# The high and low parts of z1 and z2 queued at the end of the pair two ahead, and the Gelus of two products behind the copies

## The chip, the cores and the metric

The kernel runs on one core of one Trainium2 chip. The metric is the device time of one execution in microseconds (us), of which the median of three runs is given: 945.27 us, from 944.91 to 945.61.

## What is computed

The reference is one layer on x (2048 x 512, float32): a Fourier mixing and then a gated MLP.

```python
h = _layernorm(x) * (1 + ca) + sa
x = x + ga * _A_ref(h, ...)            # (Cr h) Hr - (Ci h) Hi
h = _layernorm(x) * (1 + cb) + sb
z = _gelu(h @ w_in)                    # 2048 x 1792
z1, z2 = z[..., :896], _layernorm(z[..., 896:])
g = w_sp @ z2 + b_sp[:, None]          # w_sp is 2048 x 2048
out = x + gb * ((z1 * g) @ w_out)
```

The six vectors sa to gb come from silu(c) @ w_mod.

## The kernel before, in words

Every product runs in float32 from two rounded parts of each operand. The **high part** is a copy in a rounded type, made by ScalarE (ACT, `ah`, line 278). The **low part** is what the copy lost, made by VectorE (DVE, `al`, line 296). TensorE (PE) then runs three matmuls: high by high, high by low, low by high (lines 95 to 97).

The program is written in stages. First come the Fourier products (`gp`, `yp`, tiles numbered 0 to 127). Then come z1 = gelu(h w1) (`z1p`, tiles 128 to 155) and z2 = gelu(h w2) (`z2p`, tiles 156 to 183), then w_sp times z2 (`gw`, tiles from 184), then the output product (`op`). z1, z2 and w_sp are each done as seven products of half-size blocks instead of eight (Strassen's scheme), in the order YPROD = 1, 2, 6, 7, 4, 5, 3 for z1, and ZPROD = 1, 6, 7, 4, 5, 3, 2 for z2.

In z1 and z2 a product takes two **pairs** of moving tiles. Pair n is tiles n and n+1 (n even), so z1 has the pairs 128, 130, ... 154 and z2 the pairs 156, ... 182. A pair of z1 is 18 matmuls into three banks of PSUM (`z1p`), besides some groups of six into a fourth (`f7p`). A pair of z2 is 24 matmuls into four banks (`z2p`). A product that goes on adding to a bank needs the old sum copied out first, or put back in.

Four kinds of work stand on ACT and DVE around a pair:

- Forming the tile. For products 6 of z1 and 1 and 2 of z2 the tile is first a sum or difference on DVE (`form_t`; `s2` in line 241, `t` in line 247). For product 7 of z1 it is the first half of h with `s2` added to it (`sum_x11`, line 253, in the tiles `xb`).
- The high part (`prep_hi`, ACT) and the low part (`prep_lo`, DVE). The pools hold four high parts (`ah`, bufs=4) and three low ones, with a slot for the fourth. So the high part of tile n+4 goes where that of tile n was, and has to wait until pair n has run.
- The weights' high and low parts, one per product: `vj` (lines 633 and 637) in z1, `wj` (lines 669 and 673) in z2, in two buffers.
- Emptying the banks (`empty_z1`, `empty_z`). Products 1, 6 and 7 copy the sums out on ACT (lines 737, 771). Products 2 and 4 apply the Gelu (lines 699, 773). Products 5 and 3 add on DVE (lines 743, 775) and then apply the Gelu on ACT (lines 701, 778). After product 2 of z1 and within product 3 of z2, ACT puts an older sum back into the bank (lines 730 and 777).

The order on each engine is the order in which the program is written (`manual_schedule`). `prep(n)`, at the head of the loop's step n, queues the high part of tile n+3 and the low part of n+2, and the even steps also the low part of n+3. So the parts of pair n+4 come behind everything that empties pair n. The table `fill` (`at(n, f, ...)`, run by `run(n)`) puts the rest in: the weights' parts, the sums of w_sp's blocks (`sum_s`, `sj`), the layernorm of z2 (`norm_z`, statistics on DVE and GpSimd; `scale_z`, ACT, line 119), the parts of w_sp's first four tiles (`first`, tiles 184 to 187) and the first parts of z2 as an operand (`hi_b`, `lo_b`, called `bh` and `bl`).

Of the kernel before, what the change touches and what calls it, by code (L numbers as in the profile page):

```python
# [8 lines left out]
F32 = mybir.dt.float32  # L9
# [4 lines left out]
P = 128  # L14
# [5 lines left out]
def fnet_gmlp_kernel(  # L20
# [36 lines left out]
    Q = 512  # L57
# [8 lines left out]
    def pool(name, side="left", bufs=1):  # L66
        return tc.tile_pool(name=name, bufs=bufs, side=side, reuse_waits="tile")
# [6 lines left out]
    blocks = ctx.enter_context(pool("blocks"))  # L74
# [48 lines left out]
    def at(n, f, *a):  # L123
        fill.setdefault(n, []).append((f, a))
# [6 lines left out]
    def quad(a, r, k):  # L131
        return a[r * Q:(r + 1) * Q, k * Q:(k + 1) * Q]
# [6 lines left out]
    N2 = 4 * len(src)  # L139
    YPROD = (1, 2, 6, 7, 4, 5, 3)  # L140
    NY = {p: N2 + 4 * i for i, p in enumerate(YPROD)}
    N3 = N2 + 4 * len(YPROD)
    ZPROD = (1, 6, 7, 4, 5, 3, 2)
    NZ = {p: N3 + 4 * i for i, p in enumerate(ZPROD)}
    N4 = N3 + 4 * len(ZPROD)
# [3 lines left out]
    NB0 = len(src) + 2  # L149
    stage, T, AH, AL = {}, {}, {}, {}  # L150
# [14 lines left out]
    def load(b):  # L165
# [10 lines left out]
        elif 4 * (b - NB0) < NE - N4:  # L176
# [4 lines left out]
            for r in range(2):  # L181
                load_half(stage[b][:, r], s_d[S_OF[p], r, g] if p in S_OF else
                          quad(w_sp, r + (2 if p == 4 else 0), g + (2 if p == 1 else 0)), h)

    def squares(dst, block, k):
        nc.vector.transpose(dst.rearrange("p (b i) -> p b i", i=32), block[:, :, 32 * k:32 * k + 32])  # L186

# [9 lines left out]
    def slot(i, name, dtype=F32):  # L197
        return slots[0].tile([P, Q], dtype, tag=f"slot{i}", bufs=1, name=name)
# [56 lines left out]
    highs, lows, SE = set(), set(), []  # L255
# [8 lines left out]
    def prep_hi(n):  # L264
        if n >= NE or n in highs:
            return
        highs.add(n)
        if N2 <= n < N4:
            T[n] = form_t(n)
        else:  # L270
            b, k = divmod(n, 4) if n < N2 else (NB0 + (n - N4) // 4, (n - N4) % 4)
            T[n] = SE[1][:, k] if b == NB0 else blocks.tile([P, Q], F32, tag="t", bufs=2, name=f"t{n}")
            if n >= N4:
                squares(T[n], stage[b][:, k % 2], k // 2)
            else:
                squares(T[n], stage[b], k)
        AH[n] = SE[2][:, n - N4] if N4 <= n < N4 + 4 else blocks.tile([P, Q], F32R, tag="ah", bufs=4, name=f"ah{n}")
        nc.scalar.activation(AH[n], T[n], AF.Copy)  # L278
        if not N2 <= n < N4 and k == 3:
            stage.pop(b)  # L280
            if b != NB0:
                load(b + 2)


    def prep_lo(n):
        if n >= NE or n in lows:
            return
        lows.add(n)
        if N2 <= n < N4 and n % 4 == 3:
            AL[n] = slot(0, f"al{n}", F32R) if slots else zrow[0].tile([P, Q], F32R, tag="z1u", bufs=6, name=f"al{n}")  # L290
        elif N4 <= n < N4 + 4:
            AL[n] = slot(9 + n - N4, f"al{n}", F32R)
        else:
            AL[n] = blocks.tile([P, Q], F32R, tag="al", bufs=3, name=f"al{n}")
        t = T.pop(n)
        nc.vector.tensor_tensor(AL[n], t, AH[n].bitcast(F32), op=ALU.subtract)  # L296
        gg, kk = divmod(n % 4, 2)
        if NY[7] <= n < NY[7] + 4:
            nc.vector.tensor_tensor(TT[2 + kk, gg], TT[2 + kk, gg], S2[gg, kk], op=ALU.subtract)
# [302 lines left out]
    z_hi, z_lo, Z, ZN = {}, {}, {}, {}  # L602
# [61 lines left out]
    def w_of(p):  # L664
        return parts_w2()[{1: 0, 6: 0, 7: 1, 5: 1, 2: 2, 4: 0, 3: 3}[p]]
# [5 lines left out]
    def lo_w(p):  # L671
        hi, lo = WJ[p][:, 0, :, :ZP], WJ[p][:, 1, :, :ZP]
        nc.vector.tensor_tensor(lo, w_of(p), hi.bitcast(F32), op=ALU.subtract)

    ZB = (0, 1, 2, 6, 3, 4, 5, 7)
    Z1 = {}

    def mm_f7(g, k, th, tl):

        if k == 0:  # L680
            ZT["f7", g] = bank(6 + g % 2, f"f7p{g}")
        matmul3(ZT["f7", g], W7[0][:, 0, k], W7[0][:, 1, k], th, tl, k == 0, k == ND - 1)
        if k == ND - 1:
            end_z1(g, NF - 1, ZT.pop(("f7", g)), out_row(g, NF - 1))
# [9 lines left out]
    def turned(z):  # L694
        return z.rearrange("p (k a i) -> p k a i", k=4, i=32)
# [12 lines left out]
    def mm_z1(n):  # L708
        p = YPROD[(n - N2) // 4]
        gg = n % 4 // 2  # L710
        fresh = p in (1, 5)
        a = [(AH.pop(m), AL.pop(m)) for m in (n, n + 1)]
        if p in (2, 3):
            for kk, t in enumerate(a):
                mm_f7(gg if p == 2 else 2 + gg, 2 + kk, *t)
        for f in range(3):
            if fresh:
                ZT[gg, f] = bank(3 * gg + f, f"z1p{p}_{gg}{f}")
            cols = slice(f * P, (f + 1) * P)
            for kk, (th, tl) in enumerate(a):  # L720
                matmul3(ZT[gg, f], WJ[1, p][:, 0, kk, cols], WJ[1, p][:, 1, kk, cols], th, tl,
                        fresh and kk == 0, kk == 1, not fresh)
        for f in range(3):
            empty_z1(p, gg, f)
        if p == 1:
            for kk, t in enumerate(a):
                mm_f7(gg, kk, *t)
        if p == 2:
            for f in range(3):
                nc.scalar.activation(turned(ZT[gg, f]), natural(Z1.pop((1, gg, f))), AF.Copy)  # L730
# [15 lines left out]
    def mm_z2(n):  # L746
        p = ZPROD[(n - N3) // 4]
        gg = (n - N3) % 4 // 2
        fresh = p in (1, 5)
        a = [(AH.pop(m), AL.pop(m)) for m in (n, n + 1)]  # L750
        for r in range(4):
            q = 4 * gg + r
            ts = slice(r * P, (r + 1) * P)
            if fresh:
                ZT[q] = bank(ZB[q], f"z2p{p}_{q}")
            for kk, (th, tl) in enumerate(a):
                matmul3(ZT[q][:, :ZP], th[:, ts], tl[:, ts], WJ[p][:, 0, kk, :ZP], WJ[p][:, 1, kk, :ZP],
                        fresh and kk == 0, kk == 1, not fresh)
        empty_z(p, gg)

    def empty_z(p, gg):

        qs = range(4 * gg, 4 * gg + 4)
        for q in qs:
            if p in (1, 7):
                s = q + (8 if p == 1 else 0)
                Z[s] = zpool[s // 8].tile([P, FH], F32, name=f"z2_{s}")
            z = Z[q + (8 if p in (1, 6, 3, 2) else 0)]
            ps = ZT[q][:, :ZP]
            if p in (1, 6, 7):  # L770
                nc.scalar.activation(z[:, E0 if p == 1 else E1], ps, AF.Copy)
            elif p in (2, 4):
                nc.scalar.activation(z[:, E0], ps, AF.Gelu_apprx_tanh)
            else:
                nc.vector.tensor_tensor(z[:, E1], ps, z[:, E1], op=ALU.add)
                if p == 3:
                    nc.scalar.activation(ps, z[:, E0], AF.Copy)
                nc.scalar.activation(z[:, E1], z[:, E1], AF.Gelu_apprx_tanh)

    def norm_z(s):  # L780
# [56 lines left out]
    def mm_w(n):  # L837
# [4 lines left out]
        if k == 0 and fresh:  # L842
            for f in range(nf):
                GW[r, f] = bank(ZB[4 * r + f], f"gw{p}_{r}_{f}")
        ah, al = AH.pop(n), AL.pop(n)
# [157 lines left out]
    for s, n in ((4, 4), (5, 4), (6, 6), (7, 6), (8, 10), (9, 10)):  # L1003
        m = n + (s == 9)
# [23 lines left out]
    for j, turn, weigh, row, fold, hi in ((0, (25, 26, 27, 28), (29, 29, 30, 30), 26, (34, 34, 35, 36), (38, 35, 36, 37)),  # L1028
# [8 lines left out]
        n = weigh[3] + (3 if j == 0 else 1)  # L1037
# [13 lines left out]
    for t in range(NQ):  # L1051
        n = 8 * NQ * (t + 1)
# [86 lines left out]
    for n in range(N2, N3):  # L1139
        prep(n)  # L1140
        if n % 2 == 0:
            prep_lo(n + 3)
        run(n)
        if n % 2 == 0:
            mm_z1(n)
            if n == N2:
                prep_hi(N2 + 4)
                prep_hi(N2 + 5)
                norm_y(NQ - 1, 3)
                prep_lo(N2 + 4)  # L1150
                prep_lo(N2 + 5)
                post_h(NQ - 1, 3)
                turn_h(NQ - 1, 3)
                change_s()
                zout.append(w0.enter_context(pool("zout")))
            if n in (N2 + 6, N2 + 10):
                mm_x((n - N2) // 10)
# [9 lines left out]
    at(N3 + 6, form_w, 4)  # L1167
    at(N3 + 8, load_first)
    for k in range(4):
        at(N3 + 12 + k, prep_hi, N4 + k)  # L1170
        at(N3 + 13 + k, prep_lo, N4 + k)
    at(N4 - 8, load, NB0 + 1)
    at(N4 - 3, load, NB0 + 2)
    for i, p in enumerate(PROD):
        for k in range(8):
            n = NB[p] + 2 * k
            early = 1 if p == 1 and k == 0 else 0
            at(n - (3 if p == 1 else 4) - early, hi_b, p, k)
            at(n - 2 - early, lo_b, p, k)
            if p == 1:  # L1180
                at(n - (10 if k == 0 else 5), norm_z, k)
                at(n - (7 if k == 0 else 4), scale_z, k)
                at(n + 6, norm_z, 8 + k)
                at(n + 7, scale_z, 8 + k)
                at(n + 10, sum_t23, k)
            if p == 4:
                at(n - 5, sum_t14, k)
    for f in range(NF):
        n = N4 + 24 + 8 * f
# [4 lines left out]
    for n in range(N3, N4):  # L1194
        prep(n)
        if (n - N3) % 2 == 0:
            prep_lo(n + 3)
        run(n)
        if (n - N3) % 2 == 0:
            mm_z2(n)  # L1200

    opool = []

# [93 lines left out]
```

## Time and profile before

| | |
|---|---|
| median of three runs | 945.27 us (944.91 to 945.61) |
| the profiled execution's own time | 945.57 us |
| its span, first to last instruction | 943.8 us |
| mean granted clock of TensorE | 0.999 |
| busy: PE, DVE, ACT, GpSimd (POOL) | 934.0, 738.4, 413.9, 195.1 us |
| z1 on PE | from 448.50 to 517.17 us |
| z2 on PE | from 517.17 to 591.14 us |

A row of the timeline has the start in us from the span's start, the duration, the engine, the line of the kernel, the operation, out<-in by the program's names (without buffer numbers), the shapes and how many like it stand in a row (x2, x3). In brackets stands the engine's idle time before it, and what ended it. Matmuls overlap, so the time of one is the distance from its start to the next one's, not its duration.

### The profile page before, as it was taken

Reading aid. Unit: us, or ns where it says so; the run is one execution under the profiler, and the core shown is the slowest. Engines: PE = TensorE matmul, PEld = TensorE weight load, DVE = VectorE, ACT = ScalarE, POOL = GpSimd, SP = SyncE. Lnnn points to the kernel's source line nnn. Section 1 sums busy time; section 2 is a strip of 40 time slices with the busy share of each in tenths; the row PEclk is TensorE's granted clock in tenths of the full one; section 3 lists DMA queues with packets and bytes.
Section 4 is the critical chain, followed back from the end, with each engine's and each line's share of the span. In section 5 each row is a group of like instructions: output and inputs, shape, how many; then the busy total and the mean of one; then the engine's idle time right before and its main releaser. Section 6 shows DMA issues by size and latency. Waiting matters only on the chain.

```text
span 943.8 us, 12366 instructions
## 1 busy us (share of the span) xinstructions
PE 934.0 (99%) x4114; PEld 771.6 (82%) x4114; DVE 738.4 (78%) x1201; ACT 413.9 (44%) x726; POOL 195.1 (21%) x372
## 2 busy tenths in 40 slices
PE   8999999999999999999999998999999999999998
PEld 5888888888888888888878996888888888888886
DVE  7789957777677677866898878799799889886662
ACT  4685424232132222322686867675545444331221
POOL 2330000114553165323524200332000000000000
PEclk9999999999999999999999999999999999999999
DMA  9995762647539977994787422344554465743541
GB/s 210 221 222 123 140 145 67 167 134 189 136 101 319 272 214 209 280 334 157 232 305 275 158 69 63 93 94 105 137 133 114 108 150 134 183 110 143 182 175 57
DMA packets 236592, 157.07 MB, mean 166 GB/s; under 512 B 131472, under 2 KB 203408, under 8 KB 236400
## 3 DMA queue, kind: packets, MB, share of 16 engines
q1 hardware_dynamic: 223008, 118.65, 50.5%
q0 software_dynamic: 12128, 37.11, 10.9%
q8 instruction: 32, 0.52, 0.2%
q10 hardware_dynamic: 1392, 0.52, 0.2%
q14 instruction: 32, 0.26, 0.1%
HBM read 119.54 MB, written 36.70 MB: 166 GB/s over the span
## 4 chain that ended last, share of the span: by engine, by line
PE 93%; ACT 3%; DVE 2%; issue 1%; DMA 1%; POOL 0%; SPq 0%; DVEq 0%; ACTq 0%
PE gp L97 12%; PE gp L95 12%; PE gp L96 12%; PE gw L97 10%; PE gw L95 10%; PE gw L96 10%; PE yp L95 3%; PE yp L97 3%; PE yp L96 3%; PE op L97 3%; PE op L96 3%; PE op L95 3%; PE z1p L96 2%; PE z1p L97 2%; PE z1p L95 2%; PE z2p L97 1%
## 5 line engine op out<-in xcount | busy, mean ns | idle before, releaser
L278 ACT ACTIVATE ah<-t 128x512 fp32r<-128x512 f32 x244 | 154.0, 632 | 366.7 <-DVE t L186 238.0
L296 DVE TENSOR_TENSOR al<-t,ah 128x512 fp32r<-128x512 f32 x244 | 164.6, 675 | 67.5 <-PE gp L96 39.4
L95 PE MATMUL gp<-ah,hh 128*128 128x512 f32 x496 | 193.0, 389 | 0.0
L97 PE MATMUL gp<-ah,hl 128*128 128x512 f32 x496 | 192.9, 389 | 0.0
L96 PE MATMUL gp<-al,hh 128*128 128x512 f32 x496 | 192.9, 389 | 0.0
L186 DVE STREAM_TRANSPOSE t<-stage 128x512 f32<-128x512 f32 x236 | 165.9, 703 | 8.3 <-DMA stage<-in_A_dft_seq_re_dram 3.8
L96 PE MATMUL gw<-al,bh 128*128 128x512 f32 x400 | 155.6, 389 | 0.0
L97 PE MATMUL gw<-ah,bl 128*128 128x512 f32 x384 | 149.5, 389 | 0.0
L95 PE MATMUL gw<-ah,bh 128*128 128x512 f32 x384 | 149.4, 389 | 0.0
L96 PEld LDWEIGHTS gp<-al,hh 128*128 128x128 f32 x496 | 93.1, 188 | 19.4
L95 PEld LDWEIGHTS gp<-ah,hh 128*128 128x128 f32 x496 | 93.1, 188 | 19.4
L97 PEld LDWEIGHTS gp<-ah,hl 128*128 128x128 f32 x496 | 93.1, 188 | 19.3
L96 PEld LDWEIGHTS gw<-al,bh 128*128 128x128 f32 x400 | 75.1, 188 | 15.5
L97 PEld LDWEIGHTS gw<-ah,bl 128*128 128x128 f32 x384 | 72.1, 188 | 15.3 <-DVE bl L835 0.3
L95 PEld LDWEIGHTS gw<-ah,bh 128*128 128x128 f32 x384 | 72.1, 188 | 15.0
L807 POOL DMA_DIRECT2D s_d<-sj x64 | 35.1, 548 | 101.3 <-DVE sj L799 84.3
L95 PE MATMUL yp<-hth,gh 128*128 128x512 f32 x128 | 49.8, 389 | 0.0
L96 PE MATMUL yp<-htl,gh 128*128 128x512 f32 x128 | 49.8, 389 | 0.0
L97 PE MATMUL yp<-hth,gl 128*128 128x512 f32 x128 | 49.8, 389 | 0.0
L598 POOL DMA_DIRECT2D ht_d<-hturn x62 | 40.9, 665 | 23.6 <-DVE hturn L594 19.6
L95 PE MATMUL z2p<-wj,ah 128*128 128x448 f32 x112 | 41.5, 370 | 2.4 <-ACT ah L278 2.4
L95 PE MATMUL op<-woh,uh 128*128 128x512 f32 x112 | 43.6, 389 | 0.0
(220 smaller groups left out, 1471.2 us busy)
## 6 DMA issues: line engine op xcount, KB each, us to landing
stage<-in_A_dft_seq_im_dram SPq DMA_DIRECT2D x64, 256.0 KB, 5.3
sj<-in_B_w_sp_dram SPq DMA_DIRECT2D x32, 512.0 KB, 7.2
s_d<-sj POOLq DMA_DIRECT2D x64, 256.0 KB, 3.9
stage<-s_d SPq DMA_DIRECT2D x128, 128.0 KB, 2.8
stage<-in_A_dft_seq_re_dram SPq DMA_DIRECT2D x60, 256.0 KB, 5.3
stage<-in_B_w_sp_dram SPq DMA_DIRECT2D x88, 128.0 KB, 3.0
wm<-in_w_mod_dram SPq DMA_DIRECT2D x16, 256.0 KB, 5.7
xr<-in_A_x_dram POOLq DMA_DIRECT2D x16, 256.0 KB, 4.3
```

Of the source, the lines that this page charges most:

```text
L95: nc.tensor.matmul(acc, ah, bh, start=first, stop=False, skip_group_check=go_on)
L96: nc.tensor.matmul(acc, ah, bl, start=False, stop=False, skip_group_check=go_on)
L97: nc.tensor.matmul(acc, al, bh, start=False, stop=last, skip_group_check=go_on)
L186: nc.vector.transpose(dst.rearrange("p (b i) -> p b i", i=32), block[:, :, 32 * k:32 * k + 32])
L278: nc.scalar.activation(AH[n], T[n], AF.Copy)
L296: nc.vector.tensor_tensor(AL[n], t, AH[n].bitcast(F32), op=ALU.subtract)
L598: eng.dma_start(v[a, i], ht[32 * a:32 * a + 32].rearrange("c (b r) -> c b r", r=32))
L807: nc.gpsimd.dma_start(s_d[m, r, g][b * P:(b + 1) * P, :], a)
```

## The change

1. A new helper `ahead(n)` calls `prep_hi` for tiles n+4 and n+5 inside `mm_z1` and `mm_z2`, right behind the pair's matmuls and in front of what empties the pair. In `mm_z1` the pair 134 is left out, whose parts come behind its emptying. The low parts of n+4 and n+5 are queued right behind the emptying of pair n. A tile that has to be formed on DVE is formed where its high part is queued, so earlier too.
2. In `empty_z` the Gelus of products 5 and 3 come behind all four additions and, in product 3, behind all four copies into the banks; before, they alternated.
3. The transposes of `first` become a step of their own (`turn_first`), and they and the two parts come one or two steps earlier.
4. The statistics and scaling of z2's row block 1, and its parts `bh` and `bl`, come one to three steps earlier.

```diff
+    def turn_first(k):
+        T[N4 + k] = SE[1][:, k]
+        squares(T[N4 + k], stage[NB0][:, k % 2], k // 2)
...
-            T[n] = SE[1][:, k] if b == NB0 else blocks.tile([P, Q], F32, tag="t", bufs=2, name=f"t{n}")
-            if n >= N4:
+            if b != NB0:
+                T[n] = blocks.tile([P, Q], F32, tag="t", bufs=2, name=f"t{n}")
+            if b == NB0:
+                assert n in T
+            elif n >= N4:
                 squares(T[n], stage[b][:, k % 2], k // 2)
...
+    def ahead(n):
+        for m in (n + 4, n + 5):
+            prep_hi(m)
...
+        if n != N2 + 6:
+            ahead(n)
         for f in range(3):
             empty_z1(p, gg, f)
...
+        ahead(n)
         empty_z(p, gg)
...
                 if p == 3:
                     nc.scalar.activation(ps, z[:, E0], AF.Copy)
+        if p in (5, 3):
+            for q in qs:
+                z = Z[q + (8 if p == 3 else 0)]
                 nc.scalar.activation(z[:, E1], z[:, E1], AF.Gelu_apprx_tanh)
...
             mm_z1(n)
+            ahead(n)
             if n == N2:
-                prep_hi(N2 + 4)
-                prep_hi(N2 + 5)
                 norm_y(NQ - 1, 3)
-                prep_lo(N2 + 4)
-                prep_lo(N2 + 5)
+            prep_lo(n + 4)
+            prep_lo(n + 5)
+            if n == N2:
                 post_h(NQ - 1, 3)
...
-        at(N3 + 12 + k, prep_hi, N4 + k)
-        at(N3 + 13 + k, prep_lo, N4 + k)
+        at(N3 + 10 + k, turn_first, k)
+        at(N3 + 11 + k, prep_hi, N4 + k)
+        at(N3 + 12 + k, prep_lo, N4 + k)
...
-            early = 1 if p == 1 and k == 0 else 0
+            early = 1 if p == 1 and k < 2 else 0
...
-                at(n - (10 if k == 0 else 5), norm_z, k)
-                at(n - (7 if k == 0 else 4), scale_z, k)
+                at(n - (10, 8, 5)[min(k, 2)], norm_z, k)
+                at(n - (7, 6, 4)[min(k, 2)], scale_z, k)
...
             mm_z2(n)
+            prep_lo(n + 4)
+            prep_lo(n + 5)
```

The number behind `ah` or `al` in the rows below is the tile's; the last number of a name only tells buffers apart.

**z2, ACT.** Around product 3 (pairs 176 and 178) ACT holds the copies back into the banks (`z2p5`), the Gelus (`z2_8` and on), the layernorm's scaling (`z2_0`) and the high parts of pairs 180 and 182. Before:

```order
L777 ACTIVATE z2p5_3_5351<-z2_11_4988 128x448
L778 ACTIVATE z2_11_4988<-z2_11_4988 128x448
L278 ACTIVATE ah180_5478<-t180_5476 128x512
L119 ACTIVATE z2_0_5172<-z2_0_5172,nmrz_5383,rsz_5380 128x896
L278 ACTIVATE ah181_5484<-t181_5482 128x512
L777 ACTIVATE z2p5_4_5385<-z2_12_5031 128x448
L778 ACTIVATE z2_12_5031<-z2_12_5031 128x448
L777 ACTIVATE z2p5_5_5392<-z2_13_5033 128x448
```

Of the change, the same place:

```order
L285 ACTIVATE ah180_5466<-t180_5464 128x512
L285 ACTIVATE ah181_5470<-t181_5468 128x512
L791 ACTIVATE z2p5_0_5330<-z2_8_4986 128x448
L791 ACTIVATE z2p5_1_5337<-z2_9_4988 128x448
L791 ACTIVATE z2p5_2_5344<-z2_10_4990 128x448
L791 ACTIVATE z2p5_3_5351<-z2_11_4992 128x448
L795 ACTIVATE z2_8_4986<-z2_8_4986 128x448
L795 ACTIVATE z2_9_4988<-z2_9_4988 128x448
L795 ACTIVATE z2_10_4990<-z2_10_4990 128x448
L795 ACTIVATE z2_11_4992<-z2_11_4992 128x448
L119 ACTIVATE z2_0_5176<-z2_0_5176,nmrz_5383,rsz_5380 128x896
L285 ACTIVATE ah182_5526<-t182_5524 128x512
```

The high parts 180 and 181 stood behind eight copies and Gelus, and 181 behind the scaling too; now they stand in front of all of them.

**z1, ACT.** At the end of pair 132 ACT holds the Gelus of product 2 (`z1o0`), the copies that put the sum of product 1 back (`z1p1_00` and on), and the high parts of pair 136, whose tiles `s2` are formed on DVE. Before:

```order
L699 ACTIVATE z1o0_6_4391<-f7p0_4269 128x4x4x32
L699 ACTIVATE z1o0_0_4412<-z1p1_00_4242 128x4x4x32
L699 ACTIVATE z1o0_1_4415<-z1p1_01_4249 128x4x4x32
L699 ACTIVATE z1o0_2_4418<-z1p1_02_4256 128x4x4x32
L730 ACTIVATE z1p1_00_4242<-z1_1_00_4263 128x512
L730 ACTIVATE z1p1_01_4249<-z1_1_01_4265 128x512
L730 ACTIVATE z1p1_02_4256<-z1_1_02_4267 128x512
L278 ACTIVATE ah136_4426<-s2_00_4424 128x512
L278 ACTIVATE ah137_4431<-s2_01_4429 128x512
L699 ACTIVATE z1o1_6_4450<-f7p1_4350 128x4x4x32
```

Of the change:

```order
L710 ACTIVATE z1o0_6_4391<-f7p0_4273 128x4x4x32
L285 ACTIVATE ah136_4414<-s2_00_4412 128x512
L285 ACTIVATE ah137_4418<-s2_01_4416 128x512
L710 ACTIVATE z1o0_0_4420<-z1p1_00_4242 128x4x4x32
L710 ACTIVATE z1o0_1_4423<-z1p1_01_4249 128x4x4x32
L710 ACTIVATE z1o0_2_4426<-z1p1_02_4256 128x4x4x32
L743 ACTIVATE z1p1_00_4242<-z1_1_00_4267 128x512
```

The two high parts moved in front of three Gelus and three copies. What follows (`z1o1`, the copies of pair 134, the high parts 138 and 139) keeps its order.

**z1, DVE.** Between pairs 138 and 140 DVE holds `xb` (the tiles of product 7), the low parts of pair 140, two updates of `xb1` that go with them, and the low part `vj7` of product 7's weights. Before:

```order
L253 TENSOR_TENSOR xb0_3846<-xb0_3846,s2_01_4429 128x512
L624 TENSOR_TENSOR w1_4136<-w1e_4320,w1_4136 128x2x384
L637 TENSOR_TENSOR vj7_4512<-w1_4136,vj7_4512 128x2x384
L296 TENSOR_TENSOR al140_4544<-xb0_3846,ah140_4538 128x512
L299 TENSOR_TENSOR xb1_3936<-xb1_3936,s2_00_4424 128x512
L296 TENSOR_TENSOR al141_4547<-xb0_3846,ah141_4542 128x512
L299 TENSOR_TENSOR xb1_3936<-xb1_3936,s2_01_4429 128x512
```

Of the change:

```order
L257 TENSOR_TENSOR xb0_3846<-xb0_3846,s2_01_4416 128x512
L303 TENSOR_TENSOR al140_4542<-xb0_3846,ah140_4532 128x512
L306 TENSOR_TENSOR xb1_3936<-xb1_3936,s2_00_4412 128x512
L303 TENSOR_TENSOR al141_4545<-xb0_3846,ah141_4534 128x512
L306 TENSOR_TENSOR xb1_3936<-xb1_3936,s2_01_4416 128x512
L631 TENSOR_TENSOR w1_4136<-w1e_4320,w1_4136 128x2x384
L644 TENSOR_TENSOR vj7_4512<-w1_4136,vj7_4512 128x2x384
```

The low part of the weights stood in front of the four instructions; now it stands behind them.

## The prediction

> **What bounds the kernel now.** I read the page first, then the busy times by stage, then PE's waits, then the starts of PE's pairs.
>
> ```profile
> PE 934.0 (99%) x4114; PEld 771.6 (82%) x4114; DVE 738.4 (78%) x1201; ACT 413.9 (44%) x726; POOL 195.1 (21%) x372
> ...
> PE 93%; ACT 3%; DVE 2%; issue 1%; DMA 1%; POOL 0%; SPq 0%; DVEq 0%; ACTq 0%
> ```
>
> TensorE sets the end: 93% of the chain that ended last is its matmuls. The change takes no matmul away, so it is worth the time in which PE stands still, less the standstill that it adds. The busy times of z1, then of the end of z2 (span, PE, PEld, DVE, ACT, POOL, clock, DMA share, GB/s), and PE's own waits in both:
>
> ```profile
> 448.50:517.17 68.67, 68.57 (x301) 56.16 (x300) 58.71 (x91) 49.59 (x89) 26.95 (x49) 1.00 0.77 270
> 556.64:591.14 34.50, 31.87 (x145) 26.04 (x144) 27.10 (x48) 25.87 (x49) 2.67 (x8) 1.00 0.27 62
> PE z2p L95 <- ACT ah L278: 2.4, 4, 0.8
> ```
>
> PE idles 2.6 us at the end of z2, nearly all of it waiting for high parts. DVE, at 58.7 of 68.7 us, is the fuller of the two helpers in z1. Matmuls overlap, so idle time understates a standstill; the starts of the pairs measure it. These are the first matmuls of z2's pairs 172, 174, 176, 178, 180 and 182, and of the next stage:
>
> ```profile
> 556.64 0.37 PE L95 MATMUL z2p<-wj,ah 128*128 128x448 f32 x1
> 561.60 0.37 PE L95 MATMUL z2p<-wj,ah 128*128 128x448 f32 x1
> 566.62 0.37 PE L95 MATMUL z2p<-wj,ah 128*128 128x448 f32 x1
> 572.38 0.47 PE L95 MATMUL z2p<-wj,ah 128*128 128x448 f32 x1 [0.41 <-ACT ah L278]
> 578.64 0.47 PE L95 MATMUL z2p<-wj,ah 128*128 128x448 f32 x1 [0.80 <-ACT ah L278]
> 585.85 0.47 PE L95 MATMUL z2p<-wj,ah 128*128 128x448 f32 x1 [0.82 <-ACT ah L278]
> 591.14 0.40 PE L95 MATMUL gw<-first,bh 128*128 128x512 f32 x1
> ```
>
> Pair 172 runs undisturbed in 4.96 us. The next five take 5.02, 5.76, 6.26, 7.21 and 5.29: 29.54 against 24.80, so **4.74 us** can be won in z2. In z1 the starts of pairs 136, 138, 140, 142 and 144:
>
> ```profile
> 471.62 0.39 PE L95 MATMUL z1p<-ah,vj 128*128 128x512 f32 x1
> 475.70 0.39 PE L95 MATMUL z1p<-ah,vj 128*128 128x512 f32 x1
> 481.14 0.39 PE L95 MATMUL z1p<-ah,vj 128*128 128x512 f32 x1
> 485.48 0.39 PE L95 MATMUL z1p<-ah,vj 128*128 128x512 f32 x1
> 489.97 0.39 PE L95 MATMUL z1p<-ah,vj 128*128 128x512 f32 x1
> ```
>
> Pair 136 takes 4.08 us, 0.227 a matmul. Between 138 and 140 stand six more (1.36 us). Pairs 140 and 142 take 4.34 and 4.49, so only **0.67 us** can be won in z1.
>
> **z2: what goes.** ACT's rows at pairs 176 to 182 show the cause:
>
> ```profile
> 571.71 1.13 ACT L278 ACTIVATE ah<-xb 128x512 fp32r<-128x512 f32 x2
> ...
> 574.22 0.55 ACT L777 ACTIVATE z2p<-z 128x448 f32<-128x448 f32 x1 [0.53 <-DVE z L775]
> 574.70 0.56 ACT L778 ACTIVATE z<-z 128x448 f32<-128x448 f32 x1
> ...
> 577.97 0.61 ACT L278 ACTIVATE ah<-t 128x512 fp32r<-128x512 f32 x1
> 578.49 1.12 ACT L119 ACTIVATE z<-z,nmrz,rsz 128x896 f32<-128x896 f32 x1
> 579.52 0.61 ACT L278 ACTIVATE ah<-t 128x512 fp32r<-128x512 f32 x1
> ```
>
> High parts 180 and 181 start at 577.97 and 579.52, though their buffers were free when pair 176 ended (572.38): eight copies and Gelus (3.75 us, 574.22 to 577.97) and a scaling (1.03) stood ahead. In the change they start as pair 176 ends, take 0.52 each, and the low parts follow on DVE (0.68 each, by a row of z1 further on). Both are there some 2.5 us after the earlier pair's end, and PE needs them after 4.96. They are latest in pair 182, whose low parts stand behind four additions on DVE and whose high parts stand behind the scaling: two high parts, four copies, four Gelus and a scaling are 1.04 + 3.75 + 1.03 = 5.8 us of ACT per 4.96 us pair. ACT so falls about 1 us behind there, which leaves over 1 us of room. The additions are these:
>
> ```profile
> L775 DVE TENSOR_TENSOR z<-z2p,z 128x448 f32<-128x448 f32 x12 | 6.6, 612 | 0.0
> ```
>
> Copies into banks start 1.1 us later than the pair's end and are through after some 3.0, with 4.96 allowed. The regrouped Gelus cost nothing: copy and Gelu alternate at 0.47 us today, without a pause. The last Gelus run into the next stage, whose first matmuls need their banks; by the same sums they are through 0.9 us in time. The earlier transposes, `first` parts and row block 1 move work that is done either way; its cover is the 5 us that PE no longer gives, hence the rival below of a part of the gain. I take the whole 4.74, bounded by 0 (the lags add up and PE stands as long as now) and 4.74.
>
> **z2's first eight pairs and z1's last five.** There PE never stands, so earlier high parts win nothing. They hold the copies back to 1.25 us behind a pair's end, and at the 0.47 us that one takes, four are through by 3.2. The weights' low parts come behind the pair's low parts: two high parts (0.2 after the pair's end, then 0.62), two low ones (1.2) and a `vj` (0.95) make 3.0 us against 4.08 or more. They cost 0.
>
> **z1: what is added.** ACT today, from the end of a DMA issue to high parts 138:
>
> ```profile
> 461.88 1.57 ACT L737 ACTIVATE z<-z1p 128x512 f32<-128x512 f32 x3 [3.15 <-DVE w L621]
> ...
> 464.37 1.16 ACT L214 ACTIVATE xh<-tt 128x512 fp32r<-128x512 f32 x2
> ...
> 466.62 1.59 ACT L699 ACTIVATE z1o<-z1p 128x512 f32<-128x512 f32 x3
> 468.05 1.69 ACT L730 ACTIVATE z1p<-z 128x512 f32<-128x512 f32 x3
> 469.61 1.19 ACT L278 ACTIVATE ah<-s 128x512 fp32r<-128x512 f32 x2
> ...
> 474.12 1.23 ACT L278 ACTIVATE ah<-s 128x512 fp32r<-128x512 f32 x2
> 475.17 1.22 ACT L214 ACTIVATE xbh<-tt 128x512 fp32r<-128x512 f32 x2
> ```
>
> From 461.88 to 478 ACT has no pause, so a pause put in shifts all that follows. In the change high part 136 stands at the place of the row of 466.62. DVE today:
>
> ```profile
> 465.21 0.68 DVE L217 TENSOR_TENSOR xl<-tt,xh 128x512 fp32r<-128x512 f32 x1
> ...
> 467.87 0.69 DVE L241 TENSOR_TENSOR s<-tt,tt 128x512 f32<-128x512 f32 x1
> ...
> 474.86 1.29 DVE L296 TENSOR_TENSOR al<-s,ah 128x512 fp32r<-128x512 f32 x2 [0.84 <-ACT ah L278]
> 476.07 1.29 DVE L217 TENSOR_TENSOR xbl<-tt,xbh 128x512 fp32r<-128x512 f32 x2
> ...
> 479.35 0.95 DVE L637 TENSOR_TENSOR vj<-w,vj 128x768 fp32r<-128x768 f32 x1
> 480.22 0.68 DVE L296 TENSOR_TENSOR al<-xb,ah 128x512 fp32r<-128x512 f32 x1
> ```
>
> *The wait.* Tile `s2` starts at 467.87, at the end of a chain that begins when `xh` is there (464.37 + 0.64 = 465.0; its reader starts at 465.21). The chain can move up by 0.2 at most. So the first `s2` ends at about 468.4 and the second, no longer behind `vj6`, at 469.0. High parts 136 and 137 start at 468.5 and 469.05, and the Gelu of 466.62 at 469.55. From that Gelu to high part 138 ACT has 474.12 - 466.62 - 1.04 = 6.46 us of work, so 138 starts at 476.0, 1.9 late. What is queued behind the waiting instruction: three Gelus, three copies that pair 136 needs (the first is through at 471.65, with PE due at 471.62: about 0.1), pair 134's emptying, and high parts 138.
>
> *Pair 138* is due at 475.70. Its high part is there at 476.7, and its low part 0.7 later, for the second matmul. PE stands 1.05 there, then 0.4, and loses 0.1 at each restart: 1.67. It ends at 481.45.
>
> *Pair 140.* DVE's low parts 138 shift by 1.9 us, and with them `xbl`, `xb` and `vj7`. `vj7` moreover stands behind two low parts and two updates, 4 x 0.60 = 2.4. It ended at 480.30, and now ends at 480.30 + 1.9 + 2.4 + 0.2 (the wait for high part 140) = 484.8. The pair can start at 481.45 + 1.36 = 482.81, and its third matmul, the first that reads `vj7`'s low part, is due at 483.26. PE stands 1.6, with the restart 1.7. The pair ends at 488.6 instead of 485.48.
>
> *Pair 142* finds everything there, and its 0.41 goes. So z1 ends **2.7 us** later. The bounds: at least 0, if pair 138 takes all of ACT's delay in its room and `vj7` is no later than PE; at most 4.3, if the 1.9 us delay and the 2.4 us move reach PE whole. I take 2.7, from the rows nearest to it.
>
> What hangs on the queues' order is the whole loss. The copies of pair 130's banks, at 461.88 after 3.15 us of idleness, show it: the next pair's first matmul had started by then (the row here), yet they came behind two DMA issues that had waited for DVE.
>
> ```profile
> 460.74 0.39 PE L95 MATMUL z1p<-ah,vj 128*128 128x512 f32 x1
> ```
>
> By the Trainium skill ("PSUM — Partial Sum Buffer", Engine vs sequencer instructions) the queues of ScalarE and VectorE are strict first in, first out, with which this row agrees; by that rule the six instructions behind high part 136 wait with it and the loss stands, and if ACT could overtake, the sum would be that of the first rival.
>
> **Sum.** -4.74 + 2.7 = -2.0 us. The profiled execution took 945.57 us for a span of 943.8; it would take 943.5. The median of the three runs is 0.30 below it, so I forecast **943.3**.
>
> **Rivals.**
>
> 1. *z1 loses nothing:* `s2` is ready before ACT gets to high part 136. Then the whole 0.67 + 4.74 is won: 939.9. For it: the low parts that stand ahead of that chain on DVE come earlier in the change. Against it: the rows of 464.37 and 467.87 leave no more than 0.2. Chance 0.11.
> 2. *Part of z2's gain stays behind:* ACT, at 5.8 us per pair in product 3, falls back so far that high parts or banks are late again. With 2 of the 4.74 left: 945.3. For it: 25.87 us busy of 34.50 become the same of 29.8. Against it: the room of 1 to 2 us above. Chance 0.15.
> 3. *It doesn't do what it says:* a high part cannot start before the pair two back has ended, so queueing it earlier moves nothing: 945.3. In most pairs this is so. Against it at the end of z2: row 577.97, 5.6 us after the buffer was free. Chance 0.06.
> 4. *Slower:* the wait of pair 140 repeats at the weights of products 4, 5 and 3, since each `vj` now stands behind low parts that wait for the end of the pair two back. The room is 4.08 + 0.45 - 3.0 = 1.5 us; the rival decides once DVE has more than that in front of `vj`, as two sums of `sj` (0.7 each) and one late tile would be. Three more waits of 1.7 us give 943.3 + 5.1 = 948.4. Against it: the `sj` stand behind `vj4` in the new order. Chance 0.08.
>
> **Chances and range.** The forecast has 0.60, within 942.3 to 944.5. About 0.2% (1.9 us) is what a measurement of this kernel can tell from no change, and the line of 943.4 cuts the forecast nearly in half: 0.33 of its 0.60 faster and 0.27 the same. With the rivals: faster 0.33 + 0.11 = 0.44, same 0.27 + 0.15 + 0.06 = 0.48, slower 0.08. The range runs from 941.3 (z1 loses 0.7) to 945.7 (rivals 2 and 3), and leaves out rivals 1 and 4.
>
> **What would show it.** Right: z2's pairs from 174 to 182 each 4.96 us, no wait of PE for `ah` in z2; ACT idle nearly 2 us before `ah<-s` in z1; pair 138 1 us late, and a PE wait for `vj`'s low part (third matmul) at the start of pair 140. Wrong: no wait in z1 (rival 1), waits in z2's last pairs (rival 2), or waits at the starts of pairs 144, 148 or 152 (rival 4).

## The result and the profile after

The changed kernel took 942.53 us (median of 8 runs, 942.30 to 942.81), the kernel before 945.09 beside it (8 runs, 944.75 to 945.61): a ratio of 0.9972, with a 95% interval of 0.9962 to 0.9983, or 2.56 us less. The forecast was 943.3. The profiled execution took 942.69 us for a span of 940.9, 2.88 less than that of before (945.57).

On the page of the changed kernel the busy times, then the shares of the chain that ended last:

```profile
PE 932.1 (99%) x4114; PEld 772.7 (82%) x4114; DVE 738.3 (78%) x1201; ACT 413.6 (44%) x726; POOL 195.8 (21%) x372
...
PE 92%; DVE 2%; DMA 2%; ACT 1%; POOL 1%; issue 1%; SPq 1%; DVEq 0%; ACTq 0%; POOLq 0%
```

ACT had 3% of that chain and has 1% now: from 520.17 us to the end of z2 the chain is matmuls alone, where it ran over high parts, copies and Gelus of z2 before. PE's waits from 465 us to the end of z2 (waited for: us, times, longest) show what stands in their place:

```profile
PE z1p L97 <- DVE vj L644: 1.4, 1, 1.4
PE z1p L95 <- ACT ah L285: 0.7, 1, 0.7
PE z1p L96 <- DVE al L303: 0.2, 1, 0.2
```

All three are in z1; z2 has none. The first matmuls of z1's pairs 136, 138, 140, the third of pair 140, and those of pairs 142 and 144 (start, us, [idle before <- releaser]):

```profile
471.89 0.50 PE L95 MATMUL z1p<-ah,vj 128*128 128x512 f32 x1
476.98 0.50 PE L95 MATMUL z1p<-ah,vj 128*128 128x512 f32 x1 [0.72 <-ACT ah L285]
483.08 0.39 PE L95 MATMUL z1p<-ah,vj 128*128 128x512 f32 x1
...
485.12 0.50 PE L97 MATMUL z1p<-ah,vj 128*128 128x512 f32 x1 [1.42 <-DVE vj L644]
488.89 0.39 PE L95 MATMUL z1p<-ah,vj 128*128 128x512 f32 x1
492.97 0.39 PE L95 MATMUL z1p<-ah,vj 128*128 128x512 f32 x1
```

Pair 144 starts at 492.97, 3.00 us later than before. The chain that ended last, followed back through z1 (start, us, what; some pieces left out), tells why:

```profile
464.64 0.53 ACT xh L218
...
467.86 0.69 DVE s L245
...
469.26 0.64 ACT ah L285
469.89 1.46 ACT z1o L710 x3
471.35 1.53 ACT z1p L743 x3
...
476.39 0.55 ACT ah L285
...
477.57 0.69 DVE al L303
...
484.19 0.88 DVE vj L644
485.12 0.50 PE z1p L97
```

From 464.64 to 485.12 no matmul stands on it: `xh`, `s2`, high part 137, the Gelus and copies behind it on ACT, high and low parts of pair 138, and DVE's queue down to `vj7`.

In z2 the pairs 156 to 182 now start every 4.86 us; these are the first matmuls of pairs 180 and 182 and of the next stage:

```profile
578.54 0.36 PE L95 MATMUL z2p<-wj,ah 128*128 128x448 f32 x1
583.40 0.36 PE L95 MATMUL z2p<-wj,ah 128*128 128x448 f32 x1
588.26 0.40 PE L95 MATMUL gw<-first,bh 128*128 128x512 f32 x1
```

z2 takes 68.09 us (520.17 to 588.26) where it took 73.97 (517.17 to 591.14): 5.88 less. With z1's 3.00 that is the 2.88 of the profiled execution. So z2 gained 1.14 us more than the 4.74 that the prediction had for it. The runs below show where this came from.

### The profile page after: what moved, and what is told of

It is laid out like the page before. It is cut to its first block, busy times and chain, and to the rows that moved or that the text cites. A ratio compares the mean times of both kernels' runs of the same rounds, so it can differ in the third digit from the quotient of the medians.

```text
span 940.9 us, 12362 instructions
## 1 busy us (share of the span) xinstructions
PE 932.1 (99%) x4114; PEld 772.7 (82%) x4114; DVE 738.3 (78%) x1201; ACT 413.6 (44%) x726; POOL 195.8 (21%) x372
## 4 chain that ended last, share of the span: by engine, by line
PE 92%; DVE 2%; DMA 2%; ACT 1%; POOL 1%; issue 1%; SPq 1%; DVEq 0%; ACTq 0%; POOLq 0%
PE gp L95 12%; PE gp L96 12%; PE gp L97 12%; PE gw L97 10%; PE gw L96 10%; PE gw L95 10%; PE op L96 3%; PE op L95 3%; PE op L97 3%; PE yp L97 3%; PE yp L96 3%; PE yp L95 3%; PE z2p L97 2%; PE z2p L95 2%; PE z2p L96 2%; PE z1p L97 1%
## 5 line engine op out<-in xcount | busy, mean ns | idle before, releaser
L96 PE MATMUL op<-wol,uh 128*128 128x512 f32 x112 | 43.6, 389 | 0.0
```

Source lines behind the costliest of these rows:

```text
L96: nc.tensor.matmul(acc, ah, bl, start=False, stop=False, skip_group_check=go_on)
```

## The experiments

Times are medians in us, "before" the kernel before in the same set of runs. The length of z1 runs from pair 128 to pair 144, that of z2 from pair 156 to the next stage, both in the profiled execution. Single executions of one kernel lie up to 1.8 us apart (z2 alone from 940.06 to 941.82, of which the profile shows the longest; that of `vj7` earlier took 942.74), so tenths are better read from these lengths than from the medians.

| kernel | us | before | z1 | z2 |
|---|---|---|---|---|
| before the change | 945.09 | | 41.47 | 73.97 |
| the change | 942.53 | 945.09 | 44.44 | 68.09 |
| z2 alone | 941.25 | 945.09 | 41.62 | 69.85 |
| z1 alone | 948.37 | 945.35 | 44.42 | 73.61 |
| pair 136's parts later | 940.63 | 945.09 | 42.77 | 68.09 |
| `vj7` earlier | 941.43 | 945.09 | 43.59 | 68.09 |
| both of these | 939.61 | 945.09 | 41.60 | 68.09 |
| both, and a form later | 938.75 | 945.48 | 40.80 | 68.10 |
| z2 alone, `wj6` earlier | 939.66 | 945.48 | 41.64 | 68.09 |
| before, pair 160 earlier | 945.18 | 945.48 | 41.49 | 73.63 |
| the change without its other parts | 944.69 | 945.48 | 44.42 | 70.50 |
| transposes as before | 945.04 | 945.35 | 44.60 | 70.41 |
| Gelus as before | 942.51 | 945.35 | 44.42 | 68.09 |
| row block 1 as before | 942.59 | 945.35 | 44.41 | 68.10 |

### One stage alone

z2 alone, with z1 as before the change:

```diff
 def mm_z1(n):
-        if n != N2 + 6:
-            ahead(n)
...
             mm_z1(n)
-            ahead(n)
             if n == N2:
+                prep_hi(N2 + 4)
+                prep_hi(N2 + 5)
                 norm_y(NQ - 1, 3)
-            prep_lo(n + 4)
-            prep_lo(n + 5)
-            if n == N2:
+                prep_lo(N2 + 4)
+                prep_lo(N2 + 5)
```

> z1 as before the change, z2 and the rest as in the change. Theory (the two stages add up): z1's +3.00 us goes and z2's -5.88 stays, so 945.1 - 5.9 = 939.2 us, with all fourteen z2 pairs at 4.86. Rival (the early parts of z1 are what lets z2's pairs take 4.86 instead of 4.96): only the 4.74 us of standstill goes, 940.4, with pairs from 160 on at 4.96.

It took 941.25: the theory was 2 us off. The rival had the pace right, 4.96 us for every pair behind 160, but not a wait of PE at pair 160 (5.56 us), which makes most of its 0.8. z1 lost next to nothing (41.62 for 41.47), but z2 did not keep its 5.88. DVE's rows ahead of pair 160, then PE's first three matmuls of that pair:

```profile
524.30 1.29 DVE L303 TENSOR_TENSOR al<-s,ah 128x512 fp32r<-128x512 f32 x2
525.50 0.69 DVE L818 TENSOR_TENSOR sj<-sj 128x512 f32<-128x512 f32 x1
526.23 0.69 DVE L819 TENSOR_TENSOR sj<-sj 128x512 f32<-128x512 f32 x1
526.83 1.08 DVE L680 TENSOR_TENSOR wj<-w,wj 128x896 fp32r<-128x896 f32 x1
```

```profile
527.27 0.37 PE L95 MATMUL z2p<-wj,ah 128*128 128x448 f32 x1
527.97 0.47 PE L96 MATMUL z2p<-wj,ah 128*128 128x448 f32 x1 [0.34 <-DVE wj L680]
528.28 0.37 PE L97 MATMUL z2p<-wj,al 128*128 128x448 f32 x1
```

The low part of product 6's weights (`wj6`) stands behind low parts 160 and 161 and two sums, and ends at 527.91; PE needed it at 527.47. From there on every pair took 4.96 us without a wait. z1 alone is the change with z2's edit undone, and the change's other parts too (their diffs stand further on):

```diff
-        ahead(n)
         empty_z(p, gg)
...
             mm_z2(n)
-            prep_lo(n + 4)
-            prep_lo(n + 5)
```

> z1 as in the change, z2 and the rest as before it. Theory (z1's loss is its own): 945.1 + 3.0 = 948.1, with z2's waits of the last pairs back and its pace 4.96 from the first late operand on; if the early parts of z1 bring the weights of product 6 in time, pairs 160 to 172 take 4.86 and up to 0.7 us of the loss is given back, 947.5. Rival (z1's standstill is room that z2's late operands would have used up: what PE loses there it need not lose again): 946 to 947.

It took 948.37, 3.02 more than before beside it (ratio 1.0028, 1.0018 to 1.0039). z1's loss is its own. z2's pairs 160 to 172 took 4.86, as was expected if z1's early parts bring pair 160's operands in time; but pair 174 then waited (5.37), and z2 as a whole was only 0.36 shorter. The two halves don't add up: 3.02 - 3.84 is -0.82, the whole is -2.56. The missing 1.74 us are, within the noise, what z2 alone lost to `wj6` by the traces (69.85 against 68.09, 1.76). So z1's early parts cost 3 us in z1 and, with z2's early parts, save 1.8 in z2, where they leave DVE enough of a lead for `wj6`.

### The pace of z2

In z2 alone one operation was moved, the low part of `wj6` ahead of low parts 160 and 161:

```diff
-        at(N3 + 4 * i + 1, lo_w, p)
+        at(N3 + 4 * i + (0 if p == 6 else 1), lo_w, p)
```

> The kernel with z1 as before and z2 as in the change, with one operation moved: the low part of the weights of z2's product 6 stands ahead of low parts 160 and 161 on DVE, not behind them and two sums. Theory (one operand that is late within z2 puts PE on a pace of 4.96 us a pair instead of 4.86, and it keeps that pace though nothing is late any more): the wait of 0.6 us at pair 160 goes, and pairs 160 to 182 take 4.86: 941.25 - 0.7 - 1.1 = 939.4. Rival (the pace has to do with z1's order or with what DVE and ACT do in those pairs): only the wait goes, pairs from 160 on stay at 4.96, 940.6.

It took 939.66. No wait of PE is left in z2, and all its pairs take 4.86. The busy times of the same eleven pairs, 162 to 182, of z2 alone and of this run, for the instructions on `z2p` (span, PE, PEld, DVE, ACT, clock, DMA share, GB/s):

```profile
532.83:587.39 54.56, 54.56 (x265) 49.37 (x263) 8.90 (x16) 17.65 (x39) 1.00 0.27 78
```

```profile
531.99:585.49 53.50, 53.50 (x265) 49.41 (x263) 8.90 (x16) 17.19 (x37) 1.00 0.27 79
```

The same 264 matmuls (the count has one more that reaches over the edge), PE busy throughout, the granted clock 1.00 in both, and 1.06 us between them. An operation ahead of these pairs made it: 54.56 / 264 is 206.7 ns a matmul, 53.50 / 264 is 202.7.

The kernel before, with the parts of pair 160 alone and `wj6` earlier:

```diff
+        if n == N3:
+            prep_hi(n + 4)
+            prep_hi(n + 5)
         empty_z(p, gg)
...
             mm_z2(n)
+            if n == N3:
+                prep_lo(n + 4)
+                prep_lo(n + 5)
```

with the line on `lo_w` above.

> The kernel before the change, with the parts of z2's pair 160 alone, and the low part of the weights that it reads, made earlier: high parts ahead of the emptying of pair 156, low parts at the end of that pair. Theory (a late operand sets the pace, and it stays): pairs 160 to 172 take 4.86 us in place of 4.96 though their own operations stand where they stood, the pace returns to 4.96 at pair 174, where PE waits again; the waits of the last pairs stay: 945.1 - 0.7 = 944.4. Rival (each pair's pace comes from its own operands' queueing): pair 160 alone gains 0.1, 945.0.

Up to pair 174 the pace did as expected: pairs 160 and 174 of this run and the next stage start at

```profile
526.83 0.36 PE L95 MATMUL z2p<-wj,ah 128*128 128x448 f32 x1
...
560.87 0.37 PE L95 MATMUL z2p<-wj,ah 128*128 128x448 f32 x1
...
590.73 0.39 PE L95 MATMUL gw<-first,bh 128*128 128x512 f32 x1
```

Seven pairs take 34.04 us where they took 34.70, though the six behind pair 160 were queued as before. The rival, by which each pair's pace comes from its own operands' queueing, is out. The time did not follow: 945.18 beside 945.48, a ratio of 0.9998 (0.9989 to 1.0007), nearer the rival's 945.0 than the theory's 944.4. Pair 174 comes 0.73 us earlier, has to wait for its parts, and takes 5.31 instead of 5.02; z2 as a whole is 0.34 shorter. Nor did the slow pace return there: behind the waits of pairs 174 and 176 PE went on at 0.203 us a matmul. A faster pace is worth only what the helpers can follow.

### z1's two waits

The change, with the parts of pair 136 alone in their old place:

```diff
-        if n != N2 + 6:
+        if n not in (N2 + 4, N2 + 6):
             ahead(n)
...
             mm_z1(n)
-            ahead(n)
+            if n != N2 + 4:
+                ahead(n)
...
-            prep_lo(n + 4)
-            prep_lo(n + 5)
+            if n != N2 + 4:
+                prep_lo(n + 4)
+                prep_lo(n + 5)
```

> The change, but the parts of z1 pair 136 alone stay where they were before it, behind the emptying of pair 132. Theory (ACT's wait for s2 at high part 136 is what makes pairs 136 and 138 late): their 0.36 and 1.49 us go, vj7 is earlier by about as much as the pair that waits for it, so the wait of pair 140 stays at 1.5 to 1.7: 942.5 - 1.9 = 940.6. Rival 1 (pair 138 is late because its own high parts stand behind the emptying of pair 134, wait or no wait): 942.2. Rival 2 (the wait of pair 140 comes from the same delay and not from the place of vj7): it goes too, 939.0.

It took 940.63. ACT's rows of this run from the first Gelu to high parts 136:

```profile
466.83 0.60 ACT L710 ACTIVATE z1o<-f7p 128x512 f32<-128x512 f32 x1
467.31 1.59 ACT L710 ACTIVATE z1o<-z1p 128x512 f32<-128x512 f32 x3
468.74 1.68 ACT L743 ACTIVATE z1p<-z 128x512 f32<-128x512 f32 x3
470.31 1.19 ACT L285 ACTIVATE ah<-s 128x512 fp32r<-128x512 f32 x2
```

The pause is gone, and with it the waits of pairs 136 and 138 (0.22 is left at 138). The one wait of PE that remains in z1 is that of pair 140, 1.4 us for `vj`, as in the change: PE comes to that pair 1.4 us earlier (481.64 for 483.08), and `vj7` ends 1.4 earlier (483.65 for 485.06). So the wait at pair 140 has a cause of its own. That one alone, `vj7`'s low part at the end of index 136:

```diff
-        at(N2 + 5 + 4 * i, lo_v, p)
+        at(N2 + (4 if p == 7 else 5) + 4 * i, lo_v, p)
```

> The change, with the low part of vj7 queued one index earlier on DVE, ahead of low parts 140 and 141, their updates and the form of the next weights. Theory (vj7's place in DVE's queue makes pair 140 wait): vj7 ends near 481.6 instead of 485.1, the wait of 1.58 us and its restart go, low part 140 comes at 482.5 in place of 481.5 and is still in time: 942.5 - 1.7 = 940.8. Rival (DVE is late there as a whole, and what is put behind vj7 becomes what PE waits for): low parts 140 or 141 take its place, gain 0.7 or less, 941.8 or more.

It took 941.43, between the two. In the profiled execution pair 140 takes 4.25 instead of 5.81, but pair 142 takes 4.75 instead of 4.08. DVE's and PE's rows of this run show what is late next:

```profile
484.82 0.96 DVE L631 TENSOR_TENSOR w<-w1e,w 128x768 f32<-128x768 f32 x1
485.69 1.29 DVE L257 TENSOR_TENSOR xb<-xb,s 128x512 f32<-128x512 f32 x2
...
488.97 0.69 DVE L303 TENSOR_TENSOR al<-xb,ah 128x512 fp32r<-128x512 f32 x1
```

```profile
489.71 0.50 PE L96 MATMUL z1p<-al,vj 128*128 128x512 f32 x1 [0.25 <-DVE al L303]
```

The form of product 5's weights (0.96) stands ahead of the sums that pair 142's tiles come from. So the theory had the cause of the first wait and the rival was right that something behind it takes part of its place. With both edits:

> Both edits to the change: parts of pair 136 back in their old place, vj7's low part ahead of low parts 140 and 141. Theory (two separate causes): 942.5 - 1.85 - 1.69 = 939.0, z1 ends without any stall of PE, up to 0.7 us earlier than before the change, 938.5 to 939.0. Rival (one cause with two faces): no better than the better of the two alone, 940.6 to 940.8.

It took 939.61, 1.02 better than the better of the two: two causes, as the theory had it, but for some 0.7 us that now stand at pair 142 (4.76). The form put two indices later:

```diff
-    at(N2 + 9, form_v, 5)
+    at(N2 + 11, form_v, 5)
```

> The change with both repairs (pair 136's parts in their old place, vj7's low part early) and the form of product 5's weights behind low parts 142 and 143 on DVE in place of ahead of them. Theory (what is left of z1's standstill, 0.7 us at pair 142, is DVE's queue ahead of those low parts, of which this operation is 0.95 us): the wait goes, 939.6 - 0.6 = 939.0. Rival (pair 142 waits for a bank or for its sums, which stand ahead of that form): 939.6.

It took 938.75, 6.73 less than the kernel before beside it (ratio 0.9927, 0.9914 to 0.9939): the best version here. Its z1 up to pair 144, the rest of z1 and z2, by busy times (span, PE, PEld, DVE, ACT, POOL, clock, DMA share, GB/s):

```profile
447.97:488.77 40.80, 40.80 (x181) 33.78 (x180) 35.53 (x56) 29.71 (x55) 14.10 (x25) 1.00 0.80 276
488.77:515.97 27.20, 27.20 (x121) 22.52 (x120) 24.33 (x38) 19.88 (x35) 13.48 (x25) 1.00 0.73 269
515.97:584.07 68.10, 68.10 (x338) 63.10 (x337) 54.36 (x87) 54.92 (x104) 10.81 (x21) 1.00 0.36 110
```

PE has no gap from 448 to 584 us, and z2 keeps 4.86 a pair, so it was z1's early parts and not its standstill that helped z2.

### The change's other parts

The change without its regrouped Gelus, earlier transposes and earlier second row block (the three diffs below in one):

> The change without its other parts: copies and Gelus of products 5 and 3 alternate again, the transposes of the next stage's first tiles and the second row block's scaling stand where they stood before. Theory (these parts cost and win nothing, the parts queued ahead do all of it): 942.5, within 0.5, no wait in z2. Rival (without them ACT reaches the high parts or the banks of the last pairs too late): waits of PE come back in pairs 176 to 182 or at the first matmuls of the next stage, 943.3 or more.

It took 944.69: 0.79 less than before beside it (ratio 0.9991, 0.9982 to 1.0000), so some 1.8 of the 2.56 were gone, and the theory fell. The rival's wait came, at pair 176, but what PE waits for there is neither a high part nor a bank: it is the low part of product 3's weights (1.5 us). Each part was then undone alone, the transposes by

```diff
-        at(N3 + 10 + k, turn_first, k)
-        at(N3 + 11 + k, prep_hi, N4 + k)
-        at(N3 + 12 + k, prep_lo, N4 + k)
+        at(N3 + 12 + k, turn_first, k)
+        at(N3 + 12 + k, prep_hi, N4 + k)
+        at(N3 + 13 + k, prep_lo, N4 + k)
```

> The change, with the transposes and parts of the next stage's first tiles where they stood before it. Theory (the 2.2 us that the run without the change's other parts lost come from here: with the transpose queued right ahead of its high part, ACT waits for DVE at each tile, and the high part of product 3's weights stands behind that): PE waits some 1.8 us for that weight's low part at pair 176 and keeps the slow pace behind it: 942.5 + 2.1 = 944.6. Rival (the Gelus or the row block are the cause): 942.5.

It took 945.04, 0.31 less than before beside it, which the noise covers (ratio 0.9994, 0.9986 to 1.0003). ACT's rows of this run, DVE's, and PE's at pair 176:

```profile
559.39 0.63 ACT L285 ACTIVATE first<-first 128x512 fp32r<-128x512 f32 x1 [2.58 <-DVE first L190]
561.40 0.63 ACT L285 ACTIVATE first<-first 128x512 fp32r<-128x512 f32 x1 [1.38 <-DVE first L190]
...
565.14 0.63 ACT L285 ACTIVATE first<-first 128x512 fp32r<-128x512 f32 x1 [0.33 <-DVE first L190]
```

```profile
565.81 0.69 DVE L303 TENSOR_TENSOR al<-first,first 128x512 fp32r<-128x512 f32 x1 [0.70 <-ACT first L285]
566.42 2.21 DVE L789 TENSOR_TENSOR z<-z2p,z 128x448 f32<-128x448 f32 x4
568.54 1.28 DVE L303 TENSOR_TENSOR al<-xb,ah 128x512 fp32r<-128x512 f32 x2
569.75 1.08 DVE L680 TENSOR_TENSOR wj<-w,wj 128x896 fp32r<-128x896 f32 x1
```

```profile
568.98 0.36 PE L95 MATMUL z2p<-wj,ah 128*128 128x448 f32 x1
570.88 0.47 PE L96 MATMUL z2p<-wj,ah 128*128 128x448 f32 x1 [1.54 <-DVE wj L680]
```

Each `first` high part waits for a transpose that DVE does only just then, and DVE in turn waits for the high part before it can make the low one. By these waits both engines fall behind. The high part of product 3's weights starts at 565.68 on ACT, and their low part, which PE waits for, at 569.75 on DVE, behind four additions and two low parts. In the change, whose pairs lie 0.17 earlier there, the two start at 562.50 and 565.89, and PE does not wait. So the theory had the cause, though the last step is DVE's queue and not ACT's. The slow pace that it expected did not come: pair 178 took 4.87. The rest of the loss is pair 180, which took 5.36: its weights' low part ends at 580.96, when the pair had started at 580.51.

The other two parts, undone alone:

```diff
-        if p in (5, 3):
-            for q in qs:
-                z = Z[q + (8 if p == 3 else 0)]
                 nc.scalar.activation(z[:, E1], z[:, E1], AF.Gelu_apprx_tanh)
```

> The change, with copies and Gelus of products 5 and 3 alternating again. Theory (the early transposes do it): 942.5, within 0.4, no wait in z2. Rival (Gelus between the copies hold the banks or the weights of the last pairs back): a wait of PE in pairs 176 to 182, 943.0 or more.

```diff
-            early = 1 if p == 1 and k < 2 else 0
+            early = 1 if p == 1 and k == 0 else 0
...
-                at(n - (10, 8, 5)[min(k, 2)], norm_z, k)
-                at(n - (7, 6, 4)[min(k, 2)], scale_z, k)
+                at(n - (10 if k == 0 else 5), norm_z, k)
+                at(n - (7 if k == 0 else 4), scale_z, k)
```

> The change, with the second row block's norm and scaling where they stood before it. Theory: 942.5, within 0.4, at most the pace of the last pair or two changes (0.1 each). Rival (its operations, put between the last pairs' parts, hold the last weights back): a wait of PE in pairs 180 and 182, 942.9 or more.

They took 942.51 and 942.59, with z2 at 68.09 and 68.10: neither does anything measurable here.

## Why the prediction was right, and where its working was not

- **z1's wait for `s2`.** As worked out. High part 136 waited 1.75 us (1.9 was said), started at 468.66 (468.5), and high part 138 at 476.26 (476.0). Pairs 136 and 138 together took 11.19 us instead of 9.52, the 1.67 that the prediction gave pair 138; another 0.24 came at the start of pair 136, where it had 0.1. By the Trainium skill ("PSUM — Partial Sum Buffer", Engine vs sequencer instructions) ACT's queue is strictly first in, first out; the chain of waits agrees, with six instructions standing behind high part 137, and the run with these parts in their old place took the loss away.
- **Pair 140.** As worked out: `vj7` ended at 485.06 (484.8), the pair took 5.81, 1.73 over 4.08 (1.7). The `vj7` run shows that its place made the wait. Pair 142's 0.41 went. In sum z1 lost 3.00 instead of 2.7.
- **z2's standstill.** All of the 4.74 went; no pair waits.
- **z2's pace: the step that failed.** "Pair 172 runs undisturbed in 4.96 us" was wrong. Its PE was busy without a pause, but on a slower pace; undisturbed is 4.86, as pairs 156 and 158 of the same trace took. In the kernel before the pace changed within pair 160, whose low parts were only just there (DVE's row, and PE's load of the second one as weights):

```profile
526.38 1.29 DVE L296 TENSOR_TENSOR al<-s,ah 128x512 fp32r<-128x512 f32 x2
527.73 0.19 PEld L97 LDWEIGHTS z2p<-wj,al 128*128 128x128 f32 x1
```

  The second low part ended at 527.67, 0.06 us before that load. Up to the load's matmul (527.91) the starts lie 0.203 us apart, behind it 0.207. The weights' low part had been there since 526.46; the run with pair 160 earlier moved both operands, so that this low part alone made the pace slow is read from the trace and not shown by a run. The 4.74 was counted against a floor 0.1 a pair too high, which hid 0.49 us in the five pairs from 174 on. The other 0.65 lay in pairs 160 to 172, of which the prediction said that earlier parts win nothing there because PE never stands. Together these are the 1.14.
- **What costs nothing.** Right for the Gelus and the row block. Wrong for the transposes, taken as work that is done either way: put back, they lose 2.3 us by the traces (70.41 - 68.09). The sum came out because the change moved them too, not because they are free. Also, z1's loss and z2's gain were summed as if apart, and they are tied by `wj6`, 1.76 us: without z1's early parts z2 would have gained 4.12 (73.97 - 69.85). That the change had what z2's gain needed is luck as far as the prediction goes.
- **The fourth rival.** No wait came at products 4, 5 or 3 of z1. But its mechanism is real: a weights' low part behind low parts and two sums of `sj` is late, in z2 and with z1 as before, as the run of z2 alone shows.

The errors of size, +0.3 in z1 and -1.14 in z2, nearly make the difference between forecast and result (-0.8). The mechanism of z1's loss and of z2's waits was right; the pace, the transposes and the tie between the stages were not in the working.

## What to carry to other kernels

An instruction queued early is a gain only if its operand is early too: else it stops all that stands behind it on its engine, and each early operand pushes another back, so look for what the moved work now stands in front of. Before a stall is sized, compare the "undisturbed" stretch with other stretches of the same instruction: here a TensorE that was busy throughout ran at two paces. And a part of a change that moves work "done either way" should be undone alone before it is called free.

## What the runs showed of the hardware

- **TensorE has two steady paces** for the same stream of 128x448 matmuls with a weight load each: 202.7 and 206.7 ns, at the same granted clock of 1.00. It held the slower one for 54.56 us without a wait. In z2 the pace was seen to change only at an interruption or at an operand that came just in time. An interruption doesn't always slow it: two runs waited alike for product 3's weights in pair 176, and pair 178 then took 4.96 in the run without all other parts (575.06 to 580.02) and 4.87 in the one with the late transposes:

```profile
575.64 0.37 PE L95 MATMUL z2p<-wj,ah 128*128 128x448 f32 x1
580.51 0.36 PE L95 MATMUL z2p<-wj,ah 128*128 128x448 f32 x1
```

  What decides the pace behind an interruption stays open; the expectation above, "a late operand sets the pace, and it stays", says too much. By the Trainium skill ("TensorE: Matmul & The Clock Gate", Back-to-back issue gap) weight load and matmul set the spacing together. An estimate by its formula for an isolated gap at the full clock is 189 ns for 448 columns; both measured paces lie above it, and the section gives no second pace at an unchanged clock.
- **A restart** costs about 0.1 us beside the wait: the matmul behind a wait is listed with 0.47 to 0.50 us instead of 0.36 to 0.39, and its successor starts 0.31 later (527.97, 528.28) in place of 0.20.
